# Three attention tiles of a fused attention and gated-MLP kernel as pairs of 64-row TensorE tiles, placed inside the stretch of 64-row matmuls

## Chip, cores, metric

One core of a Trainium2 chip. The metric is the time of one execution on the device in microseconds; medians of several runs are given. All runs that are compared are in the fast state, with a granted TensorE clock of 0.998 to 1.000 of full speed; a single run of a kernel has no state of its own ("unknown"), and of such runs only the trace is used.

Words used below: PE is TensorE in the profiles, PEld its weight loads, DVE VectorE, ACT ScalarE, POOL GpSimd. PSUM is the memory that the kernel's matmuls write to, in banks; an eviction is the instruction that copies a finished result out of it. A start is the moment at which the trace has an instruction begin.

## The reference, cut to what matters

Two branches share x of 2048 rows and 512 columns and are mixed by a gate. The attention branch has 32 heads of 16 columns; per head, q and k get a softmax feature map of 32 features, the sums over the sequence are a 32x16 matrix `kv` and a 32-vector `z`, and the output is a quotient:

```python
phi_q = concat([softmax(pq), softmax(-pq)])        # 32 features of a head
kv  = einsum('bhsf,bhsd->bhfd', phi_k, v)
z   = einsum('bhsf->bhf', phi_k)
num = einsum('bhqf,bhfd->bhqd', phi_q, kv)
den = einsum('bhqf,bhf->bhq', phi_q, z)[..., None] + 1e-06
a   = (num / den) @ wo
b   = (z1 * (w_sp @ layernorm(z2) + b_sp)) @ w_out  # 688 columns in z1, z2
out = g * a + (1 - g) * b
```

## The kernel before

The sequence is cut into 16 tiles of 128 rows. The last phase handles, for each tile, the features of q (`q_tile`), half a product with `w_sp` (`gg_half`), attention (`attn_tile`) and the output product (`ba_step`). The kernel fixes the order of the instructions of TensorE and ScalarE itself; those of the other engines are ordered by the framework.

Attention of a tile is eight matmuls. Each contracts 128 rows, the 32 features of four heads, with a block-diagonal `kvz` of 68 columns: 64 of numerators and 4 of denominators. Every row has non-zero values for one head only.

```python
def attn_tile(tt):
    at = psM.tile([P, 8, P], FP32, name="at", tag="kvat", bufs=1)     # the only such PSUM tile
    for g in range(8):
        nc.tensor.matmul(at[:, g, 0:AW], lhsT=eqTs[tt][:, g, :], rhs=kvz[:, g, :],
                         start=True, stop=True)                       # AW = 68
    # ... reciprocal of the denominators, then o = at * g_el * rden, both on VectorE
    # ... o is transposed by a DMA into oTs[tt]
```

The 688 columns of u are five blocks of 128 and 48 left-over rows. The left-over rows of an even tile lie in the lower 64 partitions, those of an odd tile in the upper 64, so two tiles' matmuls can run side by side in two 64-row tiles of the TensorE array. They are kept for a group of four tiles:

```python
def ba_step(tt):
    group = next(g for g in BA_GROUPS if tt in g)    # 0-3, 4-7, 8-11, 12-13
    accs[tt] = acc_tile()
    ba_attn(accs[tt][:, :], tt, True, False)
    ba_spat(accs[tt][:, :], tt, False)
    if tt == group[-1]:
        for t in group:
            ba_rem(accs[t][:, :], t, halves[t % 2], True)   # 64 rows, 512 columns
        for t in group:
            ba_store(accs[t][:, :], t, 0, D, False)         # eviction on ScalarE, then a store

for i in range(NT - 1):
    if i + nq < NT:
        q_tile(i + nq, bank_tile(q_bank))      # nq = 6; one PSUM bank for all of them
    gg_next(...)
    attn_tile(i + 1)
    if i > 0:
        ba_step(i - 1)
```

So attention of tiles 5, 9 and 13 stands in the same pass of the loop as the left-over rows of groups 0-3, 4-7 and 8-11, some 2.3 us ahead of them.

The softmax here doesn't subtract the row's maximum and nothing guards it: scores larger than these inputs give would overflow.

Of the kernel before, what the change touches and what calls it, by code (L numbers as in the profile page):

```python
# [10 lines left out]
FP32 = mybir.dt.float32  # L11
BF16 = mybir.dt.bfloat16
I32 = mybir.dt.int32

P = 128
S = 2048
D = 512
H = 32
DH = 16
# [3 lines left out]
NT = S // P  # L23
# [5 lines left out]
NG = 4  # L29
AW = 68  # L30
# [5 lines left out]
def kernel(  # L36
# [14 lines left out]
    nc = tc.nc  # L51
# [3 lines left out]
    pers = ctx.enter_context(tc.tile_pool(name="pers", bufs=1))  # L55
    kvw = ctx.enter_context(tc.tile_pool(name="kvw", bufs=1, side="right"))
    early_cm = tc.tile_pool(name="early", bufs=1, side="right")
    early = early_cm.__enter__()
# [14 lines left out]
    mask64 = pers.tile([P, NG, DH], BF16, name="mask64")  # L73
    mask4 = pers.tile([P, NG], BF16, name="mask4")
    kvz = pers.tile([P, 8, AW], BF16, name="kvz")
    halves = [slice(64 * h, 64 * h + 64) for h in range(2)]
    bT = pers.tile([P, NT], FP32, name="bT")
    bn6 = early.tile([P, NT, 2, 6], FP32, name="bn6")
    mv = early.tile([P, NT, 2], FP32, name="mv")
    veps = early.tile([P, NT], FP32, name="veps")  # L80
    mhalf = pers.tile([P, NT], FP32, name="mhalf")
    rstd = early.tile([P, NT], FP32, name="rstd")
    glog = pers.tile([P, NT], FP32, name="glog")
    g_el = pers.tile([P, NT], FP32, name="g_el")
# [19 lines left out]
        out=ramp[:, 0, :], data0=ones32[:, :], data1=zeros[:, :], initial=0.0,  # L104
# [4 lines left out]
    for q in range(4):  # L109
        qs = slice(32 * q, 32 * q + 32)  # L110
        nc.vector.tensor_tensor(
            out=ident[qs, qs], in0=ramp[qs, 0, :], in1=ramp[qs, 1, :], op=ALU.is_equal)
# [3 lines left out]
    def load_z2w(eng, dt):  # L116
# [11 lines left out]
        out=scrap[:, :], in_=nc.const_aps.tensor(1.0, [P, 1], BF16), func=AF.Gelu_apprx_tanh)  # L128
# [5 lines left out]
    for h in range(2):  # L134
        nc.sync.dma_start(
            out=w_z1[:, 2 * h:2 * h + 2, :], in_=w_in_v[:, 2 * h:2 * h + 2, 0:FH])
    for i in range(4, 8):
        x_dma_T(i)
    for q in range(2, NCH):
        nc.sync.dma_start_transpose(  # L140
            out=xT[:, :, q * CH:(q + 1) * CH], in_=x2[q * CH:(q + 1) * CH, :]
        )
    nc.sync.dma_start(out=brow[0:NT, :], in_=B_b_sp.rearrange("(t p) -> t p", p=P))
    for qk in (1, 0):
        nc.sync.dma_start_transpose(
            out=wqkT[:, qk * NDT:(qk + 1) * NDT, :], in_=A_wqkv[:, qk * D:(qk + 1) * D])
# [4 lines left out]
    for h in range(2):  # L151
        nc.sync.dma_start(
            out=wv_sb[:, 2 * h:2 * h + 2, :],
            in_=A_wqkv[h * 2 * P:(h + 1) * 2 * P, 2 * D:3 * D].rearrange("(dt p) n -> p dt n", p=P),
        )
    for q in range(NCH):
        nc.sync.dma_start_transpose(
            out=wspT[:, :, q * CH:(q + 1) * CH], in_=B_w_sp[q * CH:(q + 1) * CH, :]
# [4 lines left out]
        out=mask4[:], in_=mask4[:], pattern=[[-32, NG]],  # L163
# [3 lines left out]
        out=mask4[:], in_=mask4[:], pattern=[[32, NG]],  # L167
# [3 lines left out]
        out=mask64[:, :, :], in_=mask4[:, :, None].to_broadcast([P, NG, DH]))  # L171
# [151 lines left out]
    with tc.manual_schedule(engines={mybir.EngineType.PE, mybir.EngineType.Activation}):  # L323
# [22 lines left out]
    psM = ctx.enter_context(  # L346
        tc.tile_pool(name="psM", bufs=1, space=bass.MemoryType.PSUM, reuse_waits="tile"))
    work = ctx.enter_context(tc.tile_pool(name="work", bufs=2, reuse_waits="tile"))
# [31 lines left out]
    def k_tile(tt):  # L380
        ek, z = expo(kvp, "ek", 5, tt, wk_p, mm_tile())
        rk = kvp.tile([P, H, 2], FP32, name="rk", bufs=3)
        nc.vector.reciprocal(out=rk[:], in_=z[:])
        even_out(ek, z, rk[:, :, 1])
        return ek, rk
# [34 lines left out]
    def kvz_evac():  # L420
# [8 lines left out]
            op0=ALU.add, op1=ALU.mult,  # L429
        )  # L430

    def load_out_weights():
        slabs = wspT[:, :, 0:D]
        w_main = [slabs[:, 0:5, :], slabs[:, 5:10, :]]
        w_rem, wo_t = slabs[:, 10, :], slabs[:, 11:11 + NDT, :]
        nc.gpsimd.memset(w_rem, 0.0)
        for h in range(2):
            gs = slice(2 * h, 2 * h + 2)
            nc.sync.dma_start(
                out=wo_t[:, gs, :],  # L440
                in_=A_wo[h * 2 * P:(h + 1) * 2 * P, :].rearrange("(g p) n -> p g n", p=P))
        for i in range(2):
            nc.sync.dma_start(
                out=w_main[i],
                in_=B_w_out[i * REM:i * REM + 5 * P, :].rearrange("(ft p) n -> p ft n", p=P),
            )
        nc.sync.dma_start(out=w_rem[0:REM, :], in_=B_w_out[5 * P:FH, :])
        nc.sync.dma_start(out=w_rem[P - REM:P, :], in_=B_w_out[0:REM, :])
        return w_main, w_rem, wo_t
# [14 lines left out]
    def attn_tile(tt):  # L464
        at = psM.tile([P, 8, P], FP32, name="at", tag="kvat", bufs=1)
        for g in range(8):
            nc.tensor.matmul(  # L467
                at[:, g, 0:AW], lhsT=eqTs[tt][:, g, :], rhs=kvz[:, g, :], start=True, stop=True)
        rden = work.tile([P, 8, NG], FP32, name="rden")
        nc.vector.reciprocal(out=rden[:], in_=at[:, :, 64:AW])  # L470
        o = work.tile([P, D], BF16, name="o")
        nc.vector.scalar_tensor_tensor(
            out=o[:].rearrange("p (u h d) -> p u h d", u=8, d=DH),
            in0=at[:, :, 0:64].rearrange("p u (h d) -> p u h d", d=DH),
            scalar=g_el[:, tt:tt + 1],
            in1=rden[:, :, :, None].to_broadcast([P, 8, NG, DH]),
            op0=ALU.mult, op1=ALU.mult,
        )
        oT = work.tile([P, NG, P], BF16, name="oT", bufs=5)
        nc.sync.dma_start_transpose(out=oT[:, :, :], in_=o[:, :])  # L480
        oTs[tt] = oT
# [6 lines left out]
    def ba_attn(acc, tt, start, stop, c0=0, c1=D):  # L488
        for g in range(NG):
            nc.tensor.matmul(acc, lhsT=oTs[tt][:, g, :], rhs=wo_t[:, g, c0:c1],  # L490
                             start=start and g == 0, stop=stop and g == NG - 1)

    def ba_spat(acc, tt, start, c0=0, c1=D):
        i = tt % 2
        for ft in range(5):
            nc.tensor.matmul(acc, lhsT=uTs[tt][:, i + ft, :], rhs=w_main[i][:, ft, c0:c1],  # L496
                             start=start and ft == 0, stop=False)

    def ba_rem(acc, tt, rows, stop, c0=0, c1=D):
        nc.tensor.matmul(  # L500
            acc, lhsT=uTs[tt][rows, 5 * (1 - tt % 2), :], rhs=w_rem[rows, c0:c1], start=False, stop=stop)

    def ba_store(acc, tt, c0, c1, on_dve):
        ob = work.tile([P, c1 - c0], BF16, name=f"ob{c1 - c0}", bufs=4 if c1 - c0 == D else 1)
        dst = out2[tt * P:(tt + 1) * P, c0:c1]
        if on_dve:
            nc.vector.tensor_scalar(
                out=ob[:, :], in0=acc, scalar1=g_inv[:, tt:tt + 1], scalar2=None, op0=ALU.mult)
            nc.sync.dma_start(out=dst, in_=ob[:, :])
        else:  # L510
            nc.scalar.activation(out=ob[:, :], in_=acc, func=AF.Copy, scale=g_inv[:, tt:tt + 1])  # L511
            nc.scalar.dma_start(out=dst, in_=ob[:, :])

    def acc_tile():
        acc_banks.append(acc_banks.pop(0))
        return bank_tile(acc_banks[-1])
# [9 lines left out]
    def ba_step(tt):  # L526
        group = next(g for g in BA_GROUPS if tt in g)
# [3 lines that stand above are left out]
        if tt == group[-1]:  # L531
            for t in group:
                ba_rem(accs[t][:, :], t, halves[t % 2], True)
            for t in group:
                ba_store(accs[t][:, :], t, 0, D, False)

# [2 lines left out]
    eqTs = {}  # L539
# [5 lines left out]
    def gg_next(gp):  # L545
        tt, j = ggs.pop(0)
        gg_half(tt, j, gp)
        if j == 1:
            uTs[tt] = u_T(tt)

    with tc.manual_schedule(engines={mybir.EngineType.PE, mybir.EngineType.Activation}):
        ks = {0: k_tile(0)}
        kvacc = psM.tile([P, 8, P], FP32, name="kvacc", tag="kvat", bufs=1)
        pend = []
        for tt in range(NT):
            if tt + 1 < NT:
                ks[tt + 1] = k_tile(tt + 1)
            ek, rk = ks.pop(tt)
            pend.append((tt, ek, v_tile(tt, rk)))
            if len(pend) == 3:  # L560
                kv_acc(*pend.pop(0))
            gg_next(mm_tile())
            if tt == 7:
                w_main, w_rem, wo_t = load_out_weights()
            if tt in Q_AT:
                q_tile(Q_AT.index(tt), mm_tile())
        nc.scalar.activation(out=g_el[:, :], in_=glog[:, :], func=AF.Exp)
        nc.vector.tensor_scalar(out=g_1p[:, :], in0=g_el[:, :], scalar1=1.0, scalar2=None, op0=ALU.add)
        nc.vector.reciprocal(out=g_inv[:, :], in_=g_1p[:, :])
        for p_ in pend:  # L570
            kv_acc(*p_)
        kvz_evac()
        gg_next(mm_tile())
        nq = len(Q_AT)
        q_bank, g_bank, *acc_banks = [next_turn("mm", 6) for _ in range(6)]
        attn_tile(0)
        for i in range(NT - 1):
            if i + nq < NT:
                q_tile(i + nq, bank_tile(q_bank))
            gg_next(bank_tile(g_bank if i + nq < NT or i % 2 == 0 else q_bank))  # L580
            attn_tile(i + 1)
            if i > 0:
                ba_step(i - 1)
        ba_tile(14)
        ba_tile(15, cuts=(0, 384, D))
# [30 lines left out]
```

## Time and profile before

| | before |
|---|---|
| median of 3 runs at first | 207.61 us (207.48 to 207.85) |
| span of the profiled run | 205.2 us |
| TensorE busy | 98% |
| attention matmuls (8 a tile) | 128 |

The page of the kernel before, its line of busy times and the two lines of the chain of work that ended last:

```profile
PE 200.5 (98%) x1522; PEld 119.9 (58%) x1540; DVE 128.5 (63%) x276; ACT 75.6 (37%) x123; POOL 45.3 (22%) x73
...
PE 95%; DMA 2%; issue 1%; ACTq 0%; DVE 0%
PE mm L454 36%; PE zp L191 18%; PE mm L359 13%; PE mm L496 8%; PE mm L399 7%; PE mm L490 7%; PE at L467 2%; PE kvacc L415 2%; DMA w_z<-in_B_w_in_dram 2%; PE mm L500 1%; PE zp L311 0%; PE pq L311 0%; PE zp L230 0%; ACTq L117 0%; ACTq L120 0%
```

TensorE is the bound: the chain is matmuls, attention (`at`) 2% of it. What TensorE waited for, by the view of waits of the kernel before (engine, line, releaser, us in total, times, longest):

```profile
PE zp L222 <- PEq L600: 0.8, 1, 0.8
```

One wait, at the start. Next, the timeline of TensorE in the first stretch of left-over rows (start in us, us, line, operation, output and inputs, shape, count); L500 are the left-over rows, L359 a q tile:

```profile
145.13 0.81 PE L496 MATMUL mm<-wspT,uT 128*128 128x512 bf16 x3
145.87 0.60 PE L500 MATMUL mm<-wspT,uT 64*128 64x512 bf16 x4
146.41 0.82 PE L359 MATMUL mm<-wq_p,xT 128*128 128x512 bf16 x3
```

and the timeline of TensorE in the pass after it, with attention of tile 6 (L467), the output product (L490, L496) and the q tile of sequence tile 12 (L359). Here and below a count can be short where the window of the query cuts a group, or where a matmul's record is missing:

```profile
149.62 0.42 PE L467 MATMUL at<-kvz,eqT 128*128 128x68 bf16 x8
149.87 1.02 PE L490 MATMUL mm<-wspT,oT 128*128 128x512 bf16 x4
150.74 1.24 PE L496 MATMUL mm<-wspT,uT 128*128 128x512 bf16 x5
151.93 1.02 PE L359 MATMUL mm<-wq_p,xT 128*128 128x512 bf16 x3
```

Read starts, not durations: the second number of a line contains a modelled end, and the next line starts before it. The eight attention matmuls hold TensorE from 149.62 to 149.87, a quarter of a microsecond. The five of L496 need 5 x 0.216 = 1.08 us at the spacing that plain 512-column matmuls show. The list of waits of the weight loads (PEld) has a trace of it, with no releaser named ("issue"), and the timeline shows the loads of that q tile standing still until the matmul starts:

```profile
PEld L359 <- issue: 0.2, 1, 0.2
```

```profile
151.93 0.53 PEld L359 LDWEIGHTS <-xT 128*128 128x128 bf16 x3 [0.23 <-issue]
```

Last, the timeline of ScalarE of the kernel before in the same pass: the fourth eviction of the group, the issue of its store, and the exponentials of q tile 11:

```profile
149.64 0.69 ACT L511 ACTIVATE ob<-mm,g_inv 128x512 bf16<-128x512 f32 x1 [0.42 <-ACT ob L511]
150.35 0.34 ACTq L512 DMA_DIRECT2D out_dram<-ob  x1
150.79 1.09 ACT L363 ACTIVATE eq<-mm 128x512 bf16<-128x512 f32 x2 [0.47 <-ACT ob L511]
```

The exponentials end at 151.88 us and the q tile starts at 151.93.

### The profile page before, as it was taken

The page shows a single profiled execution, that of the slowest core. Times are in us where ns is not written, and L with a number is a line of the kernel's source. Part 1 is how long each engine was busy: PE and PEld are TensorE (multiplying, and loading weights), DVE is VectorE, ACT ScalarE, POOL GpSimd, SP SyncE. Part 2 cuts the span into 40 slices and gives each one's busy share as a digit, 9 for nine tenths or more (in the row PEclk, how much of TensorE's full clock was granted, in tenths as well). Part 3 has the DMA queues.
Part 4 walks back from the last instruction along what each step waited for, and adds up shares of the span by engine and source line. Part 5 has one row for each costly group of instructions (what it writes and reads, how often), then busy time and mean ns, then how long its engine had stood idle before and what let it go on. Part 6 is the DMA issues. An engine that isn't in the chain of part 4 may idle for free.

```text
span 205.2 us, 3940 instructions
## 1 busy us (share of the span) xinstructions
PE 200.5 (98%) x1522; PEld 119.9 (58%) x1540; DVE 128.5 (63%) x276; ACT 75.6 (37%) x123; POOL 45.3 (22%) x73
## 2 busy tenths in 40 slices
PE   8999999999999999999999999999999999999994
PEld 4666666655665555656565666555455555665642
DVE  4467484837977597979797689555466663633330
ACT  3466678796222333342424042222351126002322
POOL 5020202021523325424242422222204220200000
PEclk9999999999999999999999999999999999999999
DMA  6998699999998027941343229763557467353542
GB/s 190 240 180 186 101 155 246 207 290 230 239 271 188 3 38 193 274 94 24 67 29 64 51 38 135 138 115 75 114 134 80 92 109 183 63 103 67 130 92 77
DMA packets 90099, 27.22 MB, mean 133 GB/s; under 512 B 84224, under 2 KB 90080, under 8 KB 90080
## 3 DMA queue, kind: packets, MB, share of 16 engines
q1 hardware_dynamic: 87312, 24.55, 63.8%
q10 hardware_dynamic: 2736, 2.42, 3.7%
q8 instruction: 12, 0.20, 0.4%
q14 instruction: 7, 0.06, 0.1%
q0 software_dynamic: 32, 0.00, 0.0%
HBM read 4.15 MB, written 2.10 MB: 30 GB/s over the span
## 4 chain that ended last, share of the span: by engine, by line
PE 95%; DMA 2%; issue 1%; ACTq 0%; DVE 0%
PE mm L454 36%; PE zp L191 18%; PE mm L359 13%; PE mm L496 8%; PE mm L399 7%; PE mm L490 7%; PE at L467 2%; PE kvacc L415 2%; DMA w_z<-in_B_w_in_dram 2%; PE mm L500 1%; PE zp L311 0%; PE pq L311 0%; PE zp L230 0%; ACTq L117 0%; ACTq L120 0%
## 5 line engine op out<-in xcount | busy, mean ns | idle before, releaser
L454 PE MATMUL mm<-z2all,wspT 128*128 128x344 bf16 x512 | 79.9, 309 | 0.0
L454 PEld LDWEIGHTS <-wspT 128*128 128x128 bf16 x512 | 49.0, 98 | 25.7 <-issue 0.4
L191 PE MATMUL zp<-w_z,xT 128*128 128x344 bf16 x252 | 37.9, 309 | 0.1
L363 ACT ACTIVATE eq<-mm 128x512 bf16<-128x512 f32 x32 | 17.4, 594 | 51.3 <-PE mm L359 25.6
L367 DVE TENSOR_REDUCE zs<-eq 128x64 f32<-128x1024 bf16 x16 | 19.5, 1220 | 20.4 <-ACT eq L363 20.4
L191 PEld LDWEIGHTS <-xT 128*128 128x128 bf16 x252 | 24.2, 98 | 12.1 <-DVE xT L290 0.5
L459 DVE SCALAR_TENSOR_TENSOR ucat<-mm,bT,z1all 128x344 bf16<-128x344 f32 x32 | 17.4, 544 | 21.9 <-PE mm L454 21.9
L376 POOL TENSOR_TENSOR eq<-eq,ratio 128x512 bf16<-128x512 bf16 x16 | 16.9, 1054 | 50.0 <-DVE ratio L375 41.8
L363 ACT ACTIVATE ek<-mm 128x512 bf16<-128x512 f32 x32 | 17.3, 600 | 27.1 <-PE mm L359 27.1
L511 ACT ACTIVATE ob<-mm,g_inv 128x512 bf16<-128x512 f32 (+1 forms) x16 | 10.9, 681 | 32.8 <-PE mm L500 26.9
L367 DVE TENSOR_REDUCE zs<-ek 128x64 f32<-128x1024 bf16 x16 | 19.3, 1209 | 2.8 <-ACT ek L363 2.8
L496 PE MATMUL mm<-wspT,uT 128*128 128x512 bf16 (+2 forms) x85 | 20.1, 367 | 0.0
L359 PEld LDWEIGHTS <-xT 128*128 128x128 bf16 x128 | 12.2, 98 | 12.9 <-PE mm L500 0.8
L376 POOL TENSOR_TENSOR ek<-ek,ratio 128x512 bf16<-128x512 bf16 x16 | 16.9, 1056 | 2.1 <-DVE ratio L375 1.5
L359 PE MATMUL mm<-wq_p,xT 128*128 128x512 bf16 x55 | 16.0, 379 | 0.5
L399 PE MATMUL mm<-wv_sb,xT 128*128 128x512 bf16 x64 | 16.4, 379 | 0.0
L359 PE MATMUL mm<-wk_p,xT 128*128 128x512 bf16 x61 | 16.1, 379 | 0.2
L490 PE MATMUL mm<-wspT,oT 128*128 128x512 bf16 (+2 forms) x62 | 15.6, 365 | 0.3
L209 DVE BATCH_NORM_STATS2 bn<-z2all 128x6 f32<-128x344 bf16 x32 | 14.9, 502 | 0.0
L206 ACT ACTIVATE z2all<-zp 128x688 bf16<-128x688 f32 x16 | 11.8, 744 | 7.4 <-PE zp L191 7.3
L264 ACT ACTIVATE z1all<-zp 128x688 bf16<-128x688 f32 x16 | 11.9, 744 | 5.1 <-PE zp L191 4.6
L496 PEld LDWEIGHTS <-uT 128*128 128x128 bf16 x85 | 8.1, 98 | 9.4 <-issue 0.2
(74 smaller groups left out, 142.5 us busy)
## 6 DMA issues: line engine op xcount, KB each, us to landing
out_dram<-ob ACTq DMA_DIRECT2D x15, 128.0 KB, 1.7
wspT<-in_B_w_out_dram SPq DMA_DIRECT2D x2, 640.0 KB, 4.9
w_z<-in_B_w_in_dram SPq DMA_DIRECT2D x2, 344.0 KB, 5.0
wv_sb<-in_A_wqkv_dram SPq DMA_DIRECT2D x2, 256.0 KB, 3.7
wspT<-in_A_wo_dram SPq DMA_DIRECT2D x2, 256.0 KB, 4.0
w_z<-in_B_w_in_dram SPq DMA_DIRECT2D x2, 172.0 KB, 3.6
xs<-in_A_x_dram SPq DMA_DIRECT2D x2, 128.0 KB, 2.5
uT<-ucat SPq DMA_TRANSPOSE x16, 2.8
```

What stands on the lines that cost most here:

```text
L191: nc.tensor.matmul(zp[:, j, 0:n], lhsT=xT[:, dt, tt * P:(tt + 1) * P], rhs=wt[:, dt, j * HF:j * HF + n], start=(dt == first), stop=(dt == ...
L209: nc.vector.bn_stats(out=bn6[:, tt, j, :], in_=z2v[:, j, :])
L264: nc.scalar.activation(out=z1all[:, tt, :].rearrange("p (j n) -> p j n", j=2), in_=zp[:, :, 0:HF], func=AF.Gelu_apprx_tanh,)
L359: nc.tensor.matmul(ps[:, :], lhsT=xT[:, dt, tt * P:(tt + 1) * P], rhs=w[:, dt, :], start=(dt == 0), stop=(dt == NDT - 1))
L363: nc.scalar.activation(out=e[:, :, a, :], in_=ps[:, :].rearrange("p (h f) -> p h f", f=DH), func=AF.Exp, scale=1.0 - 2.0 * a)
L367: nc.vector.tensor_reduce(out=z[:].rearrange("p h a -> p (h a)"), in_=e[:].rearrange("p h a f -> p (h a) f"), axis=AX.X, op=ALU.add,)
L376: nc.gpsimd.tensor_tensor(out=e[:, :, 1, :], in0=e[:, :, 1, :], in1=ratio[:, :, None].to_broadcast([P, H, DH]), op=ALU.mult)
L399: nc.tensor.matmul(v_ps[:, :], lhsT=xT[:, dt, tt * P:(tt + 1) * P], rhs=wv_sb[:, dt, :], start=(dt == 0), stop=(dt == NDT - 1))
L454: nc.tensor.matmul(gp[:, 0:HF], lhsT=wspT[:, st, tt * P:(tt + 1) * P], rhs=z2all[:, st, j * HF:(j + 1) * HF], start=(st == 0), stop=(st == ...
L459: nc.vector.scalar_tensor_tensor(out=ucat[tt % NU][:, c0 + j * HF:c0 + (j + 1) * HF], in0=gp[:, 0:HF], scalar=bT[:, tt:tt + 1], in1=z1all[ ...
L490: nc.tensor.matmul(acc, lhsT=oTs[tt][:, g, :], rhs=wo_t[:, g, c0:c1], start=start and g == 0, stop=stop and g == NG - 1)
L496: nc.tensor.matmul(acc, lhsT=uTs[tt][:, i + ft, :], rhs=w_main[i][:, ft, c0:c1], start=start and ft == 0, stop=False)
```

## The change

Intent: rows of one half (64 rows, two heads) need only 34 of the 68 columns. Two 64-row tiles of the array can work side by side, each with its own 34 columns, so that the 68 columns of a full-array matmul become two streams of 34 at the same time. Changing the array's mode costs time (in the trace of before, going into the left-over rows takes 312 ns from start to start and leaving them 308, where plain 512-column matmuls take 216), so only the tiles that can stand in a stretch that is in 64-row mode anyway are done this way. A second, narrower `kvz2` is copied on POOL; a small constant moves to another pool to make room for it.

```diff
+    kvz2 = pers.tile([P, 8, AW // 2], BF16, name="kvz2")
-    mhalf = pers.tile([P, NT], FP32, name="mhalf")
+    mhalf = early.tile([P, NT], FP32, name="mhalf")
 ... in kvz_evac:
+        for a, rows in enumerate(halves):
+            nc.gpsimd.tensor_copy(out=kvz2[rows, :, 0:32], in_=kvz[rows, :, 32 * a:32 * a + 32])
+            nc.gpsimd.tensor_copy(out=kvz2[rows, :, 32:34], in_=kvz[rows, :, 64 + 2 * a:66 + 2 * a])
 ...
+    def attn_tile_64(tt):
+        at = psM.tile([P, 2, 8, 64], FP32, name="at", tag="kvat", bufs=1)   # a PSUM bank per half
+        for g in range(8):
+            for a, rows in enumerate(halves):
+                nc.tensor.matmul(
+                    at[:, a, g, 0:AW // 2], lhsT=eqTs[tt][rows, g, :], rhs=kvz2[rows, g, :],
+                    start=True, stop=True)
 ... reciprocal and product on VectorE, once for each half instead of once
@@ in ba_step
             for t in group:
                 ba_rem(accs[t][:, :], t, halves[t % 2], True)
+            if tt + 2 < NT - 1:
+                attn_tile_64(tt + 2)
             for t in group:
                 ba_store(accs[t][:, :], t, 0, D, False)
@@ in the loop
-            attn_tile(i + 1)
+            if i not in (4, 8, 12):
+                attn_tile(i + 1)
```

More of the change, by code (lines that the diff above doesn't have):

```diff
@@ L468, in attn_tile, with o_out, o_T @@
                 at[:, g, 0:AW], lhsT=eqTs[tt][:, g, :], rhs=kvz[:, g, :], start=True, stop=True)
-        rden = work.tile([P, 8, NG], FP32, name="rden")
-        nc.vector.reciprocal(out=rden[:], in_=at[:, :, 64:AW])
+        rden = work.tile([P, 8, NG], FP32, name="rden", tag="rden")
         o = work.tile([P, D], BF16, name="o")
+        o_out(tt, o[:].rearrange("p (u h d) -> p u h d", u=8, d=DH), at[:, :, 0:AW], rden, NG)
+        o_T(tt, o)
+    def attn_tile_64(tt):
[5 more added lines that the diff above has]
+                    start=True, stop=True)
+        rden = work.tile([P, 2, 8, 2], FP32, name="rden2", tag="rden")
+        o = work.tile([P, D], BF16, name="o")
+        ov = o[:].rearrange("p (u a h d) -> p a u h d", u=8, a=2, d=DH)
+        for a in range(2):
+            o_out(tt, ov[:, a], at[:, a, :, 0:AW // 2], rden[:, a], 2)
+        o_T(tt, o)
+    def o_out(tt, o, at, rden, nh):
+        nc.vector.reciprocal(out=rden[:, :, :], in_=at[:, :, nh * DH:nh * DH + nh])
         nc.vector.scalar_tensor_tensor(
-            out=o[:].rearrange("p (u h d) -> p u h d", u=8, d=DH),
-            in0=at[:, :, 0:64].rearrange("p u (h d) -> p u h d", d=DH),
+            out=o, in0=at[:, :, 0:nh * DH].rearrange("p u (h d) -> p u h d", d=DH),
             scalar=g_el[:, tt:tt + 1],
-            in1=rden[:, :, :, None].to_broadcast([P, 8, NG, DH]),
+            in1=rden[:, :, :, None].to_broadcast([P, 8, nh, DH]),
             op0=ALU.mult, op1=ALU.mult,
         )
+    def o_T(tt, o):
         oT = work.tile([P, NG, P], BF16, name="oT", bufs=5)
```

## The prediction

> **What bounds the kernel now.** TensorE. The page gives PE 98% busy of the 205.2 us span, and the chain that ended last is 95% PE. The list of PE's waits holds one entry, 0.8 us, at the start. DVE (63%), ACT (37%) and POOL (22%) have room.
>
> **What the touched parts cost, by starts in the trace.** One attention tile is 8 full-array matmuls of 68 columns; tile 6 starts at 149.62 us and hands over at 149.87: 0.256 us, about 32 ns each (68 columns at the 344-column matmuls' 0.42 ns each are 29). Weight loads hide behind the matmuls. The left-over rows are 4 matmuls of 64 rows in pairs: the two of a pair start 3-4 ns apart, pairs 223-226 ns apart. Going into this stretch costs 312 ns after the previous 512-column start, against 216 in a plain stream (+96); leaving it 308 (+92). That agrees with the Trainium skill, "TensorEngine Tiling (Array Packing)", Key Properties: changing the mode drains TensorE, and separate tiles run in parallel. The change adds no switch, because the new pairs stand inside a stretch that is already in 64-row mode.
>
> **What the change does.** For tiles 5, 9 and 13 it removes 8 full-array matmuls (0.256 us) and adds 16 of 64 rows and 34 columns, 8 pairs. Columns streamed per row half fall from 544 to 272, but a small matmul has a floor. The weight fold (32 rows, 32 columns, four at a time) shows it: quads 25 ns apart while the queue is full, 34 ns in its steady part, so 8.5 ns of issue for each load and matmul. A pair therefore should take 17-34 ns; I take 25[...], so 8 pairs are 0.20 us (0.14 to 0.27). Saving: 0.05 us a tile, at most 0.11, hence 0.15 us in all (0 to 0.35). All of it is on the TensorE chain.
>
> **What is added off the chain.** Evacuation in halves: two reciprocals and two multiplies, estimated from 347 and 750 ns (and 195 ns for a 16-element reciprocal) at about 1.3 us instead of 1.1 per tile. DVE idles 4.05 us until 149.82, 2.2 to 3.5 us at the other two. The next attention tile needs the PSUM tile back only 3.2 us later (2.3 for tile 13), so it should not wait. The transposed o is needed by TensorE about two iterations later. Four POOL copies for the second kvz at about 120.3 us, estimated at 1-1.5 us together, push the 1.05 us scaling of one q tile back by under 1 us; that tile is not needed for over 20 us.
>
> **Prediction.** 207.61 - 0.15 gives 207.45 us, range 206.95 to 207.85. Faster by over 2%: 1%; within 2%: 98%; slower by over 2%: 1%.
>
> **What would show each step right.** Matmuls of attention in the three stretches: pair members 2-5 ns apart, pairs about 25 ns apart, the whole of 16 about 0.2 us, switch gaps still 95 ns. Full-array attention falls from 128 to 104 matmuls. PE's list of waits stays at one entry; DVE's busy time grows by about 0.6 us. The span falls by 0.1-0.2 us.
>
> **What would make it wrong.** Pairs that don't overlap (16 matmuls at 25-32 ns, 0.4-0.5 us: +0.5 us in all), a load that can't be fetched ahead of its own half's matmul (each pair 60 ns or more: +0.7 us), a wait for the single attention PSUM tile behind DVE, or a changed order of DVE or DMA work that makes TensorE wait elsewhere.

## The result, and the profile after

| | before | after |
|---|---|---|
| median, 6 runs each | 207.46 us (206.92 to 207.85) | 207.13 us (207.08 to 207.36) |
| ratio of the fast runs, 95% interval | | 0.9988 (0.9973 to 1.0003) |
| span of the profiled run | 205.2 us | 205.4 us |
| first attention matmul to last matmul, by starts in the trace | 81.668 us | 81.369 us |

Ratios are the mean time of one kernel's fast runs over that of the other's in the same rounds, so not quite the ratio of the medians. The change is within noise by the time alone: the kernel before itself scatters by 0.9 us. The profiled spans even stand the other way round. The trace separates the two. The first attention matmul of the kernel before starts at 120.497 us, that of the changed one at 120.954, so 0.46 us were lost before attention begins; at 8 us, where loads arrive, the changed kernel was already 0.59 us behind. From the first attention matmul to the last matmul the changed kernel is 0.299 us shorter, and a second profile of the changed kernel gave the same within 2 ns (see below). This time is used as the measure from here on. It is not free of scatter either: one run below has a single late transfer in it, worth 48 ns.

The same parts of the page of the changed kernel (its lines are numbered 1 to 27 higher):

```profile
PE 201.2 (98%) x1564; PEld 120.3 (59%) x1564; DVE 129.8 (63%) x282; ACT 75.4 (37%) x123; POOL 46.4 (23%) x77
...
PE 96%; DMA 2%; ACTq 0%; DVE 0%; issue 0%
```

The waits of TensorE in the changed kernel; the second is a late load at the start, over 110 us ahead of attention:

```profile
PE zp L223 <- PEq L627: 0.8, 1, 0.8
PE zp L231 <- DMA w_z<-in_B_w_in_dram: 0.5, 1, 0.5
```

What touches the attention tile in the changed kernel, by the view of that tile (minimum, median and maximum in ns, first and last start, shapes):

```profile
L472 PE MATMUL at<-kvz,eqT x104: 192/194/198, 121.0 to 195.6; 128*128 128x68 bf16 x104
L483 PE MATMUL at<-kvz,eqT x48: 173/173/177, 146.5 to 188.4; 64*128 64x34 bf16 x48
L494 DVE RECIPROCAL rden<-at x19: 248/349/353, 121.8 to 196.1; 128x32 f32<-128x32 f32 x13, 128x16 f32<-128x16 f32 x6
L495 DVE SCALAR_TENSOR_TENSOR o<-at,g_el,rden x19: 484/751/752, 122.2 to 196.5; 128x512 bf16<-128x512 f32 x13, 128x256 bf16<-128x256 f32 x6
```

104 full-array matmuls and 48 of 64 rows, as intended. The timeline of TensorE in the first stretch of the changed kernel:

```profile
145.77 0.38 PE L520 MATMUL mm<-wspT,uT 128*128 128x512 bf16 x1
146.08 0.61 PE L524 MATMUL mm<-wspT,uT 64*128 64x512 bf16 x4
146.52 0.35 PE L483 MATMUL at<-kvz,eqT 64*128 64x34 bf16 x16
146.81 1.04 PE L360 MATMUL mm<-wq_p,xT 128*128 128x512 bf16 x4
```

The stretch from L524 to the q tile takes 0.73 us (146.08 to 146.81) instead of 0.54: 0.19 us for an attention tile that took 0.256 in its old place. The single starts of the trace, in ns, show how (not a view of the profile; taken from its records):

```
left-over rows   146079 146083 | 146306 146309
attention pairs  146522 146525 | 146550 146553 | 146575 146578 | 146600 146603 | 146625 146628
                 146650 146653 | 146675 146678 | 146700 146703
next full matmul 146810
```

Two matmuls of a pair start 3 ns apart, and a pair follows the last after 25 ns. Entering the mode still costs 311 ns after a 512-column start and leaving it 107 ns after a 34-column start. That is 95 ns over the 216 ns of a plain stream, and 90 ns over an estimate of 17 ns for 34 columns (0.42 ns a column and 3 ns). The first spacing after leaving is also some 11 ns too long (227 ns instead of 216), in the kernel before as well.

And the pass after it, to be compared with the listings of before, TensorE first and then ScalarE:

```profile
150.02 0.42 PE L472 MATMUL at<-kvz,eqT 128*128 128x68 bf16 x8
150.28 1.02 PE L514 MATMUL mm<-wspT,oT 128*128 128x512 bf16 x4
151.14 1.24 PE L520 MATMUL mm<-wspT,uT 128*128 128x512 bf16 x5
152.22 1.03 PE L360 MATMUL mm<-wq_p,xT 128*128 128x512 bf16 x4
```

```profile
151.02 1.09 ACT L364 ACTIVATE eq<-mm 128x512 bf16<-128x512 f32 x2 [0.49 <-ACT ob L535]
```

Here the q tile starts 1.08 us after L520, without a gap: the exponentials end at 152.11 us, 0.11 us before TensorE gets to it. In terms of starts the gap ahead of that q tile was 331 ns before and is 216 ns now. So there are two gains on TensorE's stream: about 0.063 us in each of three stretches, 0.19 us in all, and 0.115 us of a wait that is gone. Together 0.30 us, which is what the trace shows.

### The profile page after: what moved, and what is told of

It is laid out like the page before. It is cut to its first block, busy times and chain, and to the rows that moved or that the text cites. A ratio compares the mean times of both kernels' runs of the same rounds, so it can differ in the third digit from the quotient of the medians.

```text
span 205.4 us, 4012 instructions
## 1 busy us (share of the span) xinstructions
PE 201.2 (98%) x1564; PEld 120.3 (59%) x1564; DVE 129.8 (63%) x282; ACT 75.4 (37%) x123; POOL 46.4 (23%) x77
## 4 chain that ended last, share of the span: by engine, by line
PE 96%; DMA 2%; ACTq 0%; DVE 0%; issue 0%
PE mm L459 36%; PE zp L192 18%; PE mm L360 14%; PE mm L520 8%; PE mm L514 7%; PE mm L400 7%; DMA w_z<-in_B_w_in_dram 2%; PE kvacc L416 2%; PE at L472 2%; PE mm L524 1%; PE zp L312 0%; PE at L483 0%; PE zp L231 0%; ACTq L118 0%; ACTq L121 0%; PE pq L312 0%
## 5 line engine op out<-in xcount | busy, mean ns | idle before, releaser
L520 PE MATMUL mm<-wspT,uT 128*128 128x512 bf16 (+2 forms) x85 | 20.1, 367 | 0.0
L360 PEld LDWEIGHTS <-xT 128*128 128x128 bf16 x128 | 12.2, 98 | 12.0
L514 PE MATMUL mm<-wspT,oT 128*128 128x512 bf16 (+2 forms) x68 | 16.6, 366 | 0.0
L360 PE MATMUL mm<-wq_p,xT 128*128 128x512 bf16 x64 | 16.4, 379 | 0.0
L360 PE MATMUL mm<-wk_p,xT 128*128 128x512 bf16 x64 | 16.3, 379 | 0.0
L520 PEld LDWEIGHTS <-uT 128*128 128x128 bf16 x85 | 8.1, 98 | 9.4 <-issue 0.2
```

What stands on the lines that cost most here:

```text
L360: nc.tensor.matmul(ps[:, :], lhsT=xT[:, dt, tt * P:(tt + 1) * P], rhs=w[:, dt, :], start=(dt == 0), stop=(dt == NDT - 1))
L514: nc.tensor.matmul(acc, lhsT=oTs[tt][:, g, :], rhs=wo_t[:, g, c0:c1], start=start and g == 0, stop=stop and g == NG - 1)
L520: nc.tensor.matmul(acc, lhsT=uTs[tt][:, i + ft, :], rhs=w_main[i][:, ft, c0:c1], start=start and ft == 0, stop=False)
```

## The experiments

Theory: (a) a pair of 64-row tiles costs 25 ns where the full-array matmul costs 32, and this pays only inside a stretch that is in 64-row mode anyway; (b) moving attention behind the left-over rows gave the four evictions a lead over TensorE's next work, and that took away a wait of q tile 12. Rivals: the gain is all from the move, or all from the pairs; or it comes from the new layout and copies; or it is scatter.

All nine kernels of the experiments gave right results. The measure, from the first attention matmul to the last matmul:

```
run                  us       against before   start to start into q tile 12
before               81.668                    331 ns
setup_only           81.662   -0.006           324
move_only            81.594   -0.074           216   (0.048 us of a late transfer in it)
before_one_on_dve    81.547   -0.121           215
pairs_first          81.526   -0.142           366
halves_in_turn       81.723   +0.055           215
pairs_64col          81.452   -0.216           216
after                81.369   -0.299           216
after_again          81.367   -0.301           216
kvz_first            81.366   -0.302           216
pairs_everywhere     83.154   +1.486           215
```

(215 or 216 ns is the spacing of a plain 512-column stream, so no gap.)

**after_again.** The changed kernel, unchanged.

> The changed kernel once more, for a tighter interval. Theory (pairs of 64-row tiles, 25 ns a pair, 63 ns less TensorE time per tile as the trace of the first run showed): 0.19 us less than before, ratio about 0.9991. Rival (the 0.33 us between the medians is a real gain and something beside the pairs gives the rest): ratio 0.9984. Rival (all of it is scatter): ratio 1.000.

Median 207.22 us against 207.24 for before on the same chip, ratio 0.9990 (0.9969 to 1.0011). The times cannot tell 0.9991 from 0.9984 or from 1. The trace can: 81.367 us against 81.369 in the first profile. The scatter lies ahead of the first attention matmul, which started anywhere from 120.50 to 121.21 us over the profiles, most of it decided in the first 8 us.

**move_only.** Full-array attention behind the left-over rows.

```diff
-                attn_tile_64(tt + 2)
+                attn_tile(tt + 2)
```

> Tiles 5, 9 and 13 stand behind the left-over rows, as in the change, but as full-array matmuls of 68 columns. Theory: the move alone gives nothing; each tile takes 0.25 us of TensorE wherever it stands, so the time is that of before within 0.1 us, and the trace shows the stretch from the last full matmul before the left-over rows to the first after attention 0.06 us longer than in the change. Rival (the gain comes from the move, since evictions of finished output start 0.25 us earlier): as fast as the change.

Median 207.32 us, ratio 0.9996 (0.9973 to 1.0018). In the trace the move alone gains 0.074 us, within the 0.1 us that the theory allowed, but not nothing: the timeline of TensorE shows q tile 12 without its gap, L520 at 151.41 to L360 at 152.49, 1.08 us. (The lines ahead of the dots are the first stretch.)

```profile
146.30 0.60 PE L524 MATMUL mm<-wspT,uT 64*128 64x512 bf16 x4
146.83 0.43 PE L472 MATMUL at<-kvz,eqT 128*128 128x68 bf16 x8
147.10 1.02 PE L360 MATMUL mm<-wq_p,xT 128*128 128x512 bf16 x4
...
151.41 1.24 PE L520 MATMUL mm<-wspT,uT 128*128 128x512 bf16 x5
152.49 0.81 PE L360 MATMUL mm<-wq_p,xT 128*128 128x512 bf16 x3
```

A full tile right behind the mode switch takes 0.27 us (146.83 to 147.10) instead of 0.256, but this is no loss: it is the long first spacing after leaving the mode, which the q tile has in the kernel before. What is missing from the 0.115 us was lost ahead of the move. At 128.32 us, 18 us before the first stretch, the first output product started 36 ns after its place, and its next spacing was 226 ns instead of 215. In the records the transposed `o` that it reads landed 7.147 us after the first attention matmul, 46 ns before that start; in the other ten profiles it landed at 5.5 to 7.0 us, and no such gap is there. With these 0.048 us of scatter taken out the move gains 0.122 us, as much as the wait. The stretch is 0.80 us long here against 0.73 with pairs. So (b) was found by this run: I had expected the move to be worth nothing. With setup_only (0.006) the parts add up: about 0.12 us from the move and 0.18 from the pairs make the 0.30 of the change.

**setup_only.** `kvz2` and the moved constant are there, all attention as before.

> Second kvz and the moved constant are there, attention is as before everywhere. Theory: four POOL copies, 1.2 us in all at about 120 us, that nothing on TensorE waits for: time of before within 0.1 us. Rival (the layout or the copies shift the time by themselves): a difference of 0.2 us or more either way.

81.662 us, 6 ns from before. The four POOL copies take 1.2 us together and nothing on TensorE waits for them. The median is 207.62 us, ratio 1.0012 (0.9991 to 1.0033): by the time alone this would look like 0.2 us of harm, but its profile has the difference ahead of the first attention matmul, which starts at 121.20 us against 120.50. The profile of before_one_on_dve, which has the code of before up to there, starts it at 121.21, so such a start is within the scatter. The runs do not prove that all of the 0.2 us is scatter; in the part of the kernel from the first attention matmul on, it is not found.

**pairs_everywhere.** Pairs for 12 of the other 13 tiles too, each in its ordinary place. The text below says 13, but the edit leaves tile 0, which stands ahead of the loop: the trace has 240 attention matmuls of 64 rows and 8 of the full array.

```diff
-                attn_tile(i + 1)
+                attn_tile_64(i + 1)
```

> The other 13 attention tiles too are made of 64-row pairs, each at its ordinary place between full-array matmuls. Theory: each of them saves 0.06 us in its matmuls but pays the two mode switches, estimated from the left-over rows' stretch at 0.09 us each, so it loses 0.12 to 0.13 us: 1.6 us slower than the change, 1.4 us slower than before. Rival (switches are free where no 512-column matmul has to drain, and pairs are worth it anywhere): 0.8 us faster than the change.

Median 208.80 us, ratio 1.0073 (1.0041 to 1.0106): 1.5 us slower than before, the largest effect and the only loss that the times show. The trace has 1.79 us against the change, 0.149 us for each of 12 tiles, and 1.49 us against before. The timeline of TensorE around such a tile, first of this run, then of the kernel before:

```profile
127.90 0.36 PE L483 MATMUL at<-kvz,eqT 64*128 64x34 bf16 x16
128.19 1.04 PE L514 MATMUL mm<-wspT,oT 128*128 128x512 bf16 x4
```

```profile
127.40 0.42 PE L467 MATMUL at<-kvz,eqT 128*128 128x68 bf16 x8
127.65 1.02 PE L490 MATMUL mm<-wspT,oT 128*128 128x512 bf16 x4
```

Attention to the next matmul is 0.29 us instead of 0.25 although the matmuls themselves are quicker, for it now contains the way out of the mode; and the first pair starts 242 ns after the last 344-column matmul instead of 146. Both switches cost about what they cost in the stretch (96 and 89 ns, the second against the same estimate of 17 ns). From the last matmul ahead of the tile to the output product that is 137 ns more than before, and 12 ns follow in the first spacing after leaving (225 to 228 ns instead of 215): 0.149 us together, a little over the expected 0.12 to 0.13. Pairs are worth it only where the switches are paid already.

**pairs_first.** The attention pairs ahead of the left-over rows, in the same stretch.

```diff
+            if tt + 2 < NT - 1:
+                attn_tile_64(tt + 2)
             for t in group:
                 ba_rem(accs[t][:, :], t, halves[t % 2], True)
-            if tt + 2 < NT - 1:
-                attn_tile_64(tt + 2)
```

> As the change, but in each of the three stretches the attention pairs stand ahead of the left-over rows, not behind them. Same matmuls, same mode switches; only the lead that the four evictions had over the following TensorE work is gone. From the first attention matmul to the last matmul, before took 81.668 us, the change 81.369, the move alone 81.594. Theory (0.115 us of the gain is a wait of the q tile of 12 for the exponentials of q tile 11 behind four evictions, 0.19 us is the pairs): the gap of about 330 ns ahead of that q tile's first matmul comes back, and the stretch takes 81.48 us. Rival (all 0.30 us is the pairs and their place in the mode): 81.37 us, gap 216 ns.

The gap is back, as the timeline of TensorE shows: 1.23 us from L520 to the q tile.

```profile
150.81 1.24 PE L520 MATMUL mm<-wspT,uT 128*128 128x512 bf16 x5
152.04 0.81 PE L360 MATMUL mm<-wq_p,xT 128*128 128x512 bf16 x3
```

It is 366 ns between starts, 150 ns too many, and the measure is 0.157 us over the change. 81.526 us is 0.05 above the expected 81.48, since the wait is 35 ns larger than in the kernel before and each of the three stretches 8 ns longer than in the change. Same matmuls, same switches, only the order: the lead of the evictions is what removes the wait.

**before_one_on_dve.** The kernel before, with the eviction of tile 1 moved from ScalarE to VectorE (the issue of its store leaves ScalarE with it).

```diff
-                ba_store(accs[t][:, :], t, 0, D, False)
+                ba_store(accs[t][:, :], t, 0, D, t == 1)
```

> The kernel before, with one of the four evictions after each stretch (the tile 1 only, so the first stretch alone) on VectorE, which is idle there for 4 us. Theory (the wait of the q tile of 12 comes from ScalarE's queue): ScalarE gets to the exponentials about 1.1 us sooner, the 331 ns gap ahead of that q tile is 216 ns, and from the first attention matmul to the last it takes 81.55 us instead of 81.668, without any pairs or move. Rival (the gap has another cause, a weight load or a transfer): gap stays, 81.67 us.

81.547 us, as expected. Its timeline of ScalarE, and of TensorE:

```profile
150.41 1.09 ACT L363 ACTIVATE eq<-mm 128x512 bf16<-128x512 f32 x2 [0.49 <-ACT ob L511]
```

```profile
151.44 1.24 PE L496 MATMUL mm<-wspT,uT 128*128 128x512 bf16 x5
152.52 1.03 PE L359 MATMUL mm<-wq_p,xT 128*128 128x512 bf16 x4
```

The exponentials end at 151.50 us, 1.02 us before the q tile, and the gap is gone, with no pair and no move. So the 0.115 us was a wait for ScalarE's queue of evictions. This one line gives 0.12 of the change's 0.30 us.

**halves_in_turn.** All eight matmuls of the lower rows, then all eight of the upper.

```diff
-        for g in range(8):
-            for a, rows in enumerate(halves):
+        for a, rows in enumerate(halves):
+            for g in range(8):
```

> As the change, but the 8 matmuls of the lower 64 rows are issued first, then the 8 of the upper rows. Theory (the two halves run side by side only when they alternate in issue order, and one half is bound by its weight load at 25 ns): 16 starts 25 ns apart, 0.40 us a tile instead of 0.20, from the first attention matmul to the last 81.97 us. Rival (TensorE takes the upper half ahead by itself): 81.37 us.

81.723 us, between the theory (81.97) and the rival (81.37): here the theory was half wrong. The first starts in the records, in ns:

```
lower   146113 146141 146166 146191 146216        146241 146263 146288
upper                                      146224        146266 146291 146313 146338 146363 146388 146413
```

(In a pair of close starts which is upper is put by the order. The sixth start carries the upper half's first semaphore wait, which stands ninth in program order.) One half alone goes at 25 ns a matmul, as expected. But the upper half's first matmul started ahead of three matmuls of the lower half that stand before it in the program, and three pairs overlapped; the 16 matmuls took 0.30 us, not 0.40 and not 0.18. The other two stretches show the same starts within 2 ns. So TensorE took the other half's matmul ahead here, but by three places and not by eight; alternating the halves in the program gives the full overlap.

**pairs_64col.** Seven of eight pairs stream 64 columns instead of 34 (the overhang of the neighbour's columns, into places that nobody reads).

```diff
+        kvz2f = kvz2[:].rearrange("p u c -> p (u c)")
+            nw = 64 if g < 7 else 34
-                    at[:, a, g, 0:AW // 2], lhsT=eqTs[tt][rows, g, :], rhs=kvz2[rows, g, :],
+                    at[:, a, g, 0:nw], lhsT=eqTs[tt][rows, g, :], rhs=kvz2f[rows, g * 34:g * 34 + nw],
```

> As the change, but 7 of the 8 pairs of each of the three tiles stream 64 columns instead of 34; the added columns land in places nobody reads, so the result stays right. Theory (a pair of 34 columns costs 25 ns because of its weight loads, not its columns, and the gain against 32 ns of a full-array matmul of 68 columns is only the distance to that floor): 64 columns cost 64 times 0.42 plus 2 to 3 ns, 29 to 30 ns a pair, so the 8 pairs take 0.23 us instead of 0.20 and the time from the first attention matmul to the last matmul is 81.47 us (81.369 in the change). Rival (pairs are bound by issue at 25 ns whatever their width up to 64): 81.37 us, pairs still 25 ns apart. Rival (columns count and 34 should have cost 17): a pair costs more than 34 ns.

This single run was on another chip than the other experiments (10 instead of 1). 81.452 us, 0.083 above the change, 28 ns a tile; 208 ns from the first to the eighth pair against 178, so 29.7 ns a pair. That fits the columns, 64 x 0.42 + 3 ns, as expected; at 34 the columns do not bind, as 34 x 0.42 is 14 ns and a pair takes 25. What the 25 ns are made of, the loads (the theory) or the start rate of a row half, no run tells. A single half also goes at 25 ns (halves_in_turn), and in the first part of the weight fold (32-row, 32-column matmuls, in the trace of before) four 32-row tiles went at 25 ns together; so it is not a fixed time for each matmul issued.

**kvz_first.** Beside the question: a listing of all starts over 30 ns beyond plain streaming showed the first attention matmul 64 ns late, for the second instruction that makes `kvz` stood behind a reduction on VectorE. The changed kernel with this priority:

```diff
-        kvz_evac()
+        with tc.high_priority():
+            kvz_evac()
```

> The change, with the two instructions that make kvz given priority on VectorE: the second stood behind a 1.22 us reduction, and the first attention tile started 64 ns late for it. Expected: the gap ahead of the first attention matmul falls from 210 to 146 ns, everything after it is as in the change, so from the last matmul of the kv sum to the last matmul 0.064 us less than the change. Too small for the times, whose scatter is 0.2 us.

VectorE in the changed kernel, and then in this one (timeline):

```profile
118.76 0.69 DVE L422 TENSOR_TENSOR kvz<-kvacc,mask 128x512 bf16<-128x512 f32 x1 [0.80 <-PE kvacc L416]
119.41 1.22 DVE L368 TENSOR_REDUCE zs<-eq 128x64 f32<-128x1024 bf16 x1
120.55 0.17 DVE L594 TENSOR_SCALAR g_1p<-g_el 128x16 f32<-128x16 f32 x1
120.62 0.18 DVE L427 SCALAR_TENSOR_TENSOR kvz<-kvacc,mask 128x32 bf16<-128x32 f32 x1
```

```profile
118.56 0.69 DVE L422 TENSOR_TENSOR kvz<-kvacc,mask 128x512 bf16<-128x512 f32 x1 [0.80 <-PE kvacc L416]
119.17 0.18 DVE L427 SCALAR_TENSOR_TENSOR kvz<-kvacc,mask 128x32 bf16<-128x32 f32 x1
119.27 1.21 DVE L368 TENSOR_REDUCE zs<-eq 128x64 f32<-128x1024 bf16 x1
```

From the last matmul of the kv sum to the last matmul it took 83.731 us against 83.798 in the change, 0.067 us less where 0.064 was expected; the first attention matmul no longer has a gap ahead of it. Median of 5 runs 206.84 us against 207.43 for before (9 runs), ratio 0.9968 (0.9954 to 0.9981). It is the quickest kernel and the only one whose interval against before excludes 1 on the good side; that it is quicker than the change by the time alone (206.84 against 207.13 and 207.22) was not measured side by side, and the trace accounts for 0.067 us of it. Of the 0.59 us between the medians the traces account for 0.37 (83.731 us against 84.098 in the kernel before); the rest lies ahead of that stretch and is not explained.

## Why the prediction was right

- *TensorE bounds the kernel, and only its stream counts*: right. VectorE, POOL and DMA work that the change added (next points) cost TensorE nothing.
- *A pair takes 25 ns, members 2-5 ns apart, no added switch*: right, 25 and 3 ns; the switches stay at 95 and 90 ns. Why it is 25 ns stays open (pairs_64col). *0.05 us a tile, 0.15 in all*: measured 0.063 and 0.19. The small excess: eight pairs span 0.178 us to the last start, and what follows the last pair is counted in the cost of leaving the mode, so the tile costs 0.19 and not 0.20.
- *0.15 us in all (0 to 0.35)*: on TensorE's stream the gain was 0.30 us. The missing term is 0.115 us of a wait that the prediction did not have, because it took *the list of PE's waits holds one entry* for all there is. The list goes by idle time behind modelled ends; a 512-column record lasts 379 ns while starts are 216 ns apart, so a gap under some 160 ns is hidden from it (379 - 216 = 163). The start-to-start distance shows it, and so does the list of the weight loads' waits (L359, 0.2 us, in before), though without a releaser; the entry stands in setup_only and pairs_first too, where the gap is, and in none of the traces without it. And the prediction costed the pairs but not the move, which is what removed the wait. That 0.30 us still lies in the predicted 0 to 0.35 is in part luck: the pairs' share was mis-sized by 0.04 us, and 0.115 us came from a term that was not there.
- *Evacuation at 1.3 us a tile*: 1.47 us, twice 248 + 484 ns; VectorE grew by 1.3 us in all, not by 0.6. *The next attention tile should not wait*: right; no gap ahead of it.
- *Four POOL copies, 1-1.5 us*: 1.17 us, and no wait of TensorE followed.
- *PE's list of waits stays at one entry*: it got a second, 0.5 us for a load at the start. *The span falls by 0.1-0.2 us*: the profiled span rose by 0.2, for the start-up differs from run to run by more than the gain.
- *207.45 us, 206.95 to 207.85*: 207.13 measured, inside, 0.3 us below the point. A third of a microsecond is within the scatter, and the kernel before, at 207.46 us, lies in the same range; so the time alone confirms nothing. The trace confirms the mechanism of the pairs and corrects the sum.

## What to carry to other kernels

Splitting small matmuls into row tiles paid by nanoseconds here (63 a tile), and only where the array was already in that mode; a detour into the mode for one small group cost more than it gave (149 ns a tile), so look for a stretch that has paid the switches, and alternate the halves in program order. Moving work can free a wait elsewhere: count what the move itself does to the queues of the other engines. When a gain is below the scatter of the times, measure a stretch of the trace between two fixed instructions, and read gaps from start to start, since a list of waits built on modelled ends hides short ones; look at the weight loads' waits as well. Then step through the two traces and see where the difference arises: a late transfer far from the change (move_only) can pass for an effect of it.

## What the Trainium skill lacked or had wrong

- "TensorE: Matmul & The Clock Gate", Part 3, What overlaps and what doesn't, says matmuls are "pc-monotone in start AND end". Ends were not observed here, but starts were not in program order: in halves_in_turn the ninth matmul, known by its semaphore wait, started at 146.224 us, ahead of the sixth to eighth (146.241 to 146.288).
- "TensorEngine Tiling (Array Packing)", Key Properties, says that changing the mode drains TensorE, without a figure. Here going into 64-row mode cost 94-97 ns over the plain spacing and leaving it 88-93 ns in the loop (after 34 columns against an estimated spacing of 17 ns), 103 ns in the last stretch, with some 11 ns more in the spacing after it; 0.149 us net for a tile of 16 small matmuls.
- "TensorE: Matmul & The Clock Gate", Back-to-back issue gap, gives in its table about 60 cycles, some 25 ns, for 1 to 64 columns. A row half with 34 columns agrees (25 ns, with one half or both at work), but 64 columns took 29.7 ns a pair, over the table's figure.
- "Perfetto Trace Analysis", Per-engine timelines, rightly says that TensorE's end times are estimated. It lacks the consequence: a wait of 0.115 us between 512-column matmuls was invisible as idle time of the matmuls, and showed, without a cause, as a stop of 0.23 us among the weight loads.
